# Sliding-window attention feeding a gated MLP: values cast by the loading DMA, attention outputs transposed by DMA

## The chip, the cores and the metric

The kernel runs on one core of a Trainium2 chip. The core has five engines with queues of their own: TensorE (PE, matrix products into PSUM), VectorE (DVE), ScalarE (ACT), GpSimd (POOL) and SyncE (SP, which here only issues DMAs). Sixteen DMA engines move data between HBM and SBUF; any of SyncE, ScalarE and GpSimd can issue to them. The metric is the device time of one execution in microseconds. The kernel before has a median of 345.35 us over three runs (345.25 to 346.49).

## The reference

There are 8 batches, 8 heads, 576 positions and a head size of 64. Attention is causal, sees the last 128 positions and carries a linear bias by distance with a slope for each head. Its output, one row of 512 numbers for each of the 4608 tokens, goes through two products with a gate between them.

```python
scores = scale * np.matmul(q, k.transpose(0, 1, 3, 2))
mask = (rel >= 0) & (rel < window)                     # window = 128
scores = np.where(mask, scores + bias[None], -1000000000.0)
attn = softmax(scores)                                 # written out in the reference
x = np.matmul(attn, v).transpose(0, 2, 1, 3).reshape(B * S, H * D)
# ---- then
h = x @ w_in                                           # 512 -> 2048
g = h * (1.0 / (1.0 + np.exp(-beta * h)))
out = g @ w_out                                        # 2048 -> 512
```

All inputs and the output are float32. The kernel computes its products in bfloat16 with float32 sums.

## The kernel before

The work is two streams that are woven together on TensorE. The attention stream goes batch by batch. A batch has five blocks of query positions (four of 128 and one of 64). The product stream goes in nine groups of 512 tokens: HS(g, j) makes one of 16 slices of the hidden layer, OS(g, i, n) a quarter of one of four output tiles. HS reads XT, a ring of three groups that holds the attention outputs with the features on the partitions.

Loads. Every block of q, k or v comes in as float32 by SyncE into a buffer of the pool `fst`, and GpSimd casts it to its place. Values land in VS, which is double-buffered by batch.

```python
fst_pool = ctx.enter_context(tc.tile_pool(name="fst", bufs=14))
bst_pool = ctx.enter_context(tc.tile_pool(name="bst", bufs=8))
xn_pool = ctx.enter_context(tc.tile_pool(name="xn", bufs=6))

def load_rows(src, b, sb):                  # 256 KB, rows of 256 bytes
    f = fst_pool.tile([P, H, D], F32, name="fst", tag="fst")
    nc.sync.dma_start(out=f[0:rows], in_=src[b, :, P*sb : P*sb+rows, :].rearrange("h p d -> p h d"))
    return f[0:rows]

def load_qk(b, sb):                         # batches 3 to 7
    t = bst_pool.tile([P, 2, H, D], BF16, name="bst", tag="bst")
    for i, src in enumerate((q, k)):
        c = nc.gpsimd.tensor_copy(out=t[0:ROWS[sb], i], in_=load_rows(src, b, sb))
    staged[b, sb] = t

def load_v(b, sb):
    return nc.gpsimd.tensor_copy(out=VS[b % 2][0:ROWS[sb], sb, :, 0:D], in_=load_rows(v, b, sb))
```

Transposes of q and k. In batches 0 to 2 TensorE does them. From batch 3 on TD does them by DMA, two for each block, issued by SyncE into QK, which is double-buffered by batch too.

```python
def TD(b, sb):
    src = staged.pop((b, sb))
    for i in range(2):
        nc.sync.dma_start_transpose(out=QK[b % 2][:, i, :, ...], in_=src[0:ROWS[sb], i]...)
```

Attention. SC(b, m, p) makes the scores of a pair of heads for one half of a batch and their exponentials. PV(b, qb, g) makes the weighted sum of values for four heads of block qb, and VectorE divides it. X(b, qb) turns the finished block onto XT: four transposes on TensorE, then a copy by VectorE (by ScalarE in batch 0), in two parts where the block crosses the end of the ring.

```python
def X(b, qb):
    xnv = xns.pop((b, qb))[:].rearrange("p h d -> p (h d)")
    tok0 = (b * S + P * qb) % XTR
    n1 = min(nq, XTR - tok0)
    parts = [(tok0, 0, n1)] + ([(0, n1, nq)] if n1 < nq else [])
    xt = psum_t.tile([P, NDM, P], BF16, name="xt", tag="t")
    for c in range(NDM):
        nc.tensor.transpose(out=xt[:, c, :], in_=xnv[:, c*P : (c+1)*P], identity=ident[:])
    copy = nc.vector.tensor_copy if b else nc.scalar.copy
    for at, r0, r1 in parts:
        copy(out=XT[:, :, at : at + r1 - r0], in_=xt[:, :, r0:r1])
```

The weave. TensorE's order is that of the program (a manual schedule). The order on the other engines, the DMA queue of SyncE among them, is made by a scheduler when the kernel is built; each queue is then served strictly in its order. `spread` puts the steps of a list `todo` between product steps, and leaves the last `tail` product steps without any. The `todo` of group g ends with the X that completes the tokens of group g+1. With tokens 0 to 2047 in groups 0 to 3, that is X(3, 2) for group 3.

```python
def spread(moe, todo, lead=0, tail=3): ...

def ahead(b, m):                # DMA issues, all at one place of the program
    def f():
        if m == 0:
            TD(b, 3), TD(b, 4); load_v(b, 2..4)
            if b + 1 < B: load_qk(b + 1, 0..2)
        elif b + 1 < B:
            TD(b + 1, 0..2); load_qk(b + 1, 3..4); load_v(b + 1, 0..1)
    return f

def by_block(b):                # batches 3 to 7; e is the batch before
    e = b - 1
    r = [pv(e, 2, 1), pv(e, 3, 1), x(e, 2), sc(b, 0, 0), x(e, 3), pv(e, 4, 1), sc(b, 0, 1),
         x(e, 4)] if e >= NTE else [sc(b, 0, 0), sc(b, 0, 1)]            # NTE = 3
    return [ahead(b, 0)] + r + [
        sc(b, 0, 2), pv(b, 0, 0), sc(b, 0, 3), pv(b, 1, 0), ahead(b, 1),
        pv(b, 0, 1), sc(b, 1, 0), x(b, 0), pv(b, 1, 1), sc(b, 1, 1), x(b, 1),
        sc(b, 1, 2), pv(b, 2, 0), sc(b, 1, 3), pv(b, 3, 0), pv(b, 4, 0)]

spread(hs(0), by_pair(1), 1, 0)             # batch 1 beside group 0
...                                         # hs(1) alone; batch 2 beside os(0) and half of os(1)
for g in range(2, NTG):                     # NTG = 9
    moe = ...                               # hs(g) with the rest of os(1), or with os(g - 1)
    if g + 1 < NTG:
        b, r = divmod(TOKG * (g + 2) - 1, S)
        end = todo.index(at[b, r // P]) + 1
    spread(moe, todo[done:end])
```

Output tiles are stored by GpSimd, those of the last group by SyncE.

Of the kernel before, what the change touches and what calls it, by code (L numbers as in the profile page):

```python
# [13 lines left out]
P = 128  # L14
# [3 lines left out]
def kernel(  # L18
# [10 lines left out]
    nc = tc.nc  # L29
    B, H, S, D = q.shape  # L30
# [8 lines left out]
    NTE = 3  # L39
# [36 lines left out]
    W2 = const.tile([P, NFF, DM], BF16, name="W2")  # L76
    const.seal()

    fst_pool = ctx.enter_context(tc.tile_pool(name="fst", bufs=14))
    bst_pool = ctx.enter_context(tc.tile_pool(name="bst", bufs=8))  # L80
    pt_pool = ctx.enter_context(tc.tile_pool(name="ptp", bufs=11))
    xn_pool = ctx.enter_context(tc.tile_pool(name="xn", bufs=6))
    gt_pool = ctx.enter_context(tc.tile_pool(name="gt", bufs=2))
    sig_pool = ctx.enter_context(tc.tile_pool(name="sig", bufs=3))
    osb_pool = ctx.enter_context(tc.tile_pool(name="osb", bufs=6))
# [37 lines left out]
    def load_qk(b, sb):  # L123
        t = bst_pool.tile([P, 2, H, D], BF16, name="bst", tag="bst")
        for i, src in enumerate((q, k)):
            c = nc.gpsimd.tensor_copy(out=t[0 : ROWS[sb], i], in_=load_rows(src, b, sb))  # L126
        staged[b, sb] = t
        return c

    def load_v(b, sb):  # L130
        return nc.gpsimd.tensor_copy(  # L131
            out=VS[b % 2][0 : ROWS[sb], sb, :, 0:D], in_=load_rows(v, b, sb)
        )
# [102 lines left out]
# [3 lines that stand above are left out]
            nc.sync.dma_start_transpose(  # L239
                out=QK[b % 2][:, i, :, P * sb : P * sb + ROWS[sb]],  # L240
                in_=src[0 : ROWS[sb], i].rearrange("r h d -> r (h d)"),
            )
# [80 lines left out]
    def X(b, qb):  # L323
        nq = ROWS[qb]
        xnv = xns.pop((b, qb))[:].rearrange("p h d -> p (h d)")
        tok0 = (b * S + P * qb) % XTR
        n1 = min(nq, XTR - tok0)
        parts = [(tok0, 0, n1)] + ([(0, n1, nq)] if n1 < nq else [])
        xt = psum_t.tile([P, NDM, P], BF16, name="xt", tag="t")
        for c in range(NDM):  # L330
            nc.tensor.transpose(  # L331
                out=xt[:, c, :], in_=xnv[:, c * P : (c + 1) * P], identity=ident[:]
# [4 lines that stand above are left out]
# [38 lines left out]
    def spread(moe, todo, lead=0, tail=3):  # L375
        done, n = 0, len(moe)
        for i, it in enumerate(moe):
            it()
            to = len(todo) * (i + 1 - lead) // (n - lead - tail)
            while done < min(len(todo), to):  # L380
                todo[done]()
                done += 1

    def sc(b, m, p):
        return lambda: SC(b, m, p)

    def pv(b, qb, g):
        return lambda: PV(b, qb, g)
# [6 lines left out]
    at = {}  # L395


    def ahead(b, m):
        def f():
            if m == 0:  # L400
                for sb in (3, 4):
                    TD(b, sb)
                for sb in (2, 3, 4):
                    load_v(b, sb)
                if b + 1 < B:
                    for sb in (0, 1, 2):
                        load_qk(b + 1, sb)
            elif b + 1 < B:
                for sb in (0, 1, 2):
                    TD(b + 1, sb)  # L410
                for sb in (3, 4):
                    load_qk(b + 1, sb)
                for sb in (0, 1):
                    load_v(b + 1, sb)
        return f

    def by_pair(b):
        return [
            lambda: TP(b, 0), lambda: TP(b, 1), sc(b, 0, 0), lambda: TT(b), sc(b, 0, 1),
            lambda: TP(b, 2), sc(b, 1, 0), lambda: TP(b, 3), sc(b, 1, 1), pv(b, 0, 0), sc(b, 0, 2),  # L420
            pv(b, 1, 0), sc(b, 1, 2), pv(b, 2, 0), sc(b, 0, 3), pv(b, 3, 0), sc(b, 1, 3),
            pv(b, 4, 0), pv(b, 0, 1), pv(b, 1, 1), x(b, 0), pv(b, 2, 1), x(b, 1), pv(b, 3, 1),
            x(b, 2), pv(b, 4, 1), x(b, 3), x(b, 4),
        ]

    def by_block(b):

        e = b - 1
        r = [pv(e, 2, 1), pv(e, 3, 1), x(e, 2), sc(b, 0, 0), x(e, 3), pv(e, 4, 1), sc(b, 0, 1),
             x(e, 4)] if e >= NTE else [sc(b, 0, 0), sc(b, 0, 1)]  # L430
        return [ahead(b, 0)] + r + [
            sc(b, 0, 2), pv(b, 0, 0), sc(b, 0, 3), pv(b, 1, 0), ahead(b, 1),
            pv(b, 0, 1), sc(b, 1, 0), x(b, 0), pv(b, 1, 1), sc(b, 1, 1), x(b, 1),
            sc(b, 1, 2), pv(b, 2, 0), sc(b, 1, 3), pv(b, 3, 0), pv(b, 4, 0),
        ]

    with tc.manual_schedule(engines={mybir.EngineType.PE}):

        for sb in range(NQB):
            c = load_v(0, sb)  # L440
            if sb == 3:
                with tc.issue_after(c.ins):
                    load_w1(0)
                    load_w1(1)
        for p in range(NP):
            c = load_pair(1, p, None if p else W1[0:1, 0, 0:1])
            if p % 2:
                with tc.issue_after(c.ins):
                    load_w1(2 + p // 2)
            if p == 1:  # L450
                load_tail(1)
        for sb in range(NQB):
            c = load_v(1, sb)
            if sb == 3:
                with tc.issue_after(c.ins):
                    for n in range(4):
                        load_w2(n)
        with tc.tile_pool(name="psum_x", bufs=2, space=bass.MemoryType.PSUM) as psum_x:
            pools = [psum_x, psum_x, psum_s]

            def sc0(m, p):
                SC(0, m, p, pools[0])
                pools.append(pools.pop(0))

            w = psum_t.tile([P, 512], F32, name="w", tag="t")
            idle(w[:], 9)
            TP(0, 0)
            TP(0, 1)
            sc0(0, 0)
            load_beta()  # L470
            TT(0)
            sc0(0, 1)
            TP(0, 2)
            sc0(1, 0)
            TP(0, 3)
            sc0(1, 1)
            for m in range(2):
                sc0(m, 2)
            for m in range(2):
                sc0(m, 3)  # L480
                PV(0, m, 0)
            for qb in (2, 3, 4):
                PV(0, qb, 0)
        psum_h = ctx.enter_context(
            tc.tile_pool(name="psum_h", bufs=2, space=bass.MemoryType.PSUM))
        psum_o = ctx.enter_context(
            tc.tile_pool(name="psum_o", bufs=2, space=bass.MemoryType.PSUM))
        w = psum_s.tile([P, 2, 512], F32, name="w", tag="sps")
        for qb in range(NQB):
            c = PV(0, qb, 1, (psum_o, "ops") if qb % 2 else (psum_h, "hps"))  # L490
            idle(w[:, 0, :], 1)
            if qb:
                X(0, qb - 1)
                idle(w[:, 1, :], 1)
        X(0, NQB - 1)
        with tc.issue_after(c.ins):
            late_consts()
        for p in range(NP):
            load_pair(2, p)
            if p == 1:  # L500
                load_tail(2)

        def hs(g):
            return [lambda j=j: HS(g, j) for j in range(NFF)]

        def os(g):
            return [lambda n=n: OS(g, n // 4, n % 4) for n in range(NFF)]


        spread(hs(0), by_pair(1), 1, 0)  # L510
        for sb in range(NQB):
            load_v(2, sb)
        for sb in (0, 1, 2):
            load_qk(3, sb)
        for it in hs(1):
            it()
        ahead(2, 1)()
        o1 = os(1)
        spread(os(0) + o1[0:8], by_pair(2))
        todo = sum((by_block(b) for b in range(NTE, B)), [])  # L520
        todo += [pv(B - 1, 2, 1), pv(B - 1, 3, 1), x(B - 1, 2), pv(B - 1, 4, 1), x(B - 1, 3),
                 x(B - 1, 4)]
        done = 0
        for g in range(2, NTG):
            moe = hs(g)
            if g == 2:
                moe = sum((moe[2 * n : 2 * n + 2] + [o1[8 + n]] for n in range(8)), [])
            else:
                moe = sum(([a, c] for a, c in zip(moe, os(g - 1))), [])
            end = len(todo)  # L530
            if g + 1 < NTG:
                b, r = divmod(TOKG * (g + 2) - 1, S)
                end = todo.index(at[b, r // P]) + 1
            spread(moe, todo[done:end])
            done = end
        for it in os(NTG - 1):
            it()
# [30 lines left out]
```

## Time and profile before

| | kernel before |
|---|---|
| time, median of 3 | 345.35 us |
| span of the profiled execution | 344.5 us |
| DMA queues of SyncE and ScalarE (hardware) | 119296 packets, 35.27 MB, 55.2% of 16 engines' span |
| DMA queue of GpSimd (software) | 6784 packets, 12.59 MB, 14.4% |
| transposes of attention outputs, TensorE (L331) | 160, 219 ns each |
| copies to XT, VectorE (L336) | 36, 13.8 us in all |
| casts of values, GpSimd (L131) | 40, 617 ns each |
| value loads, SyncE | 32 of 256 KB and 8 of 128 KB, 5.3 and 5.2 us to landing |
| transposes of q and k by DMA (L239) | 50, 3.2 us to landing |

A row of the page names a line of the kernel, an engine, an operation and its tiles as out<-in, then busy time, the mean of one, and the idle time of the engine before it with what ended it. "SPq" is the SyncE queue: the time there is that of issuing, not of the transfer. Matmuls overlap, so that the mean duration of one is longer than the distance between the starts of two.

### The profile page before, as it was taken

The numbers are of one execution on the slowest core, as the hardware profiler recorded it, in microseconds if no ns is written. First come the engines' busy times: TensorE is split into PE (matmuls) and PEld (weight loads), VectorE is DVE, ScalarE is ACT, GpSimd is POOL, SyncE is SP. The second block draws the span as 40 slices with busy tenths as digits, with TensorE's granted clock in tenths as the row PEclk, the third lists the DMA queues.
The fourth block names the chain that finished last, engine by engine and source line by source line (L and its number), as shares of the span: only waits on it lengthen the run. The fifth ranks groups of instructions, "written<-read, shape, count | busy, mean of one in ns | idle before, by whom it ended". The sixth has DMA issues, their size and how long they took to land.

```text
span 344.5 us, 6371 instructions
## 1 busy us (share of the span) xinstructions
PE 327.8 (95%) x2379; PEld 157.4 (46%) x2379; DVE 206.2 (60%) x447; ACT 211.5 (61%) x407; POOL 100.6 (29%) x173
## 2 busy tenths in 40 slices
PE   7988979999998999999999999999999999999995
PEld 2453434444453444444454444444544445444442
DVE  6476768776645785565677656676767456533300
ACT  4745754757618875667758774877587674444411
POOL 7635482250443434304804352200000000100000
PEclk9999999999999999999999999999999999999999
DMA  6999999999999999959999796100000000010021
GB/s 195 246 170 262 217 213 242 214 192 131 181 216 202 192 217 189 169 115 239 199 241 233 126 234 162 47 30 32 30 33 30 32 30 32 32 60 32 30 81 72
DMA packets 126143, 48.27 MB, mean 140 GB/s; under 512 B 113296, under 2 KB 123552, under 8 KB 126112
## 3 DMA queue, kind: packets, MB, share of 16 engines
q1 hardware_dynamic: 119296, 35.27, 55.2%
q0 software_dynamic: 6784, 12.59, 14.4%
q8 instruction: 18, 0.29, 0.4%
q14 instruction: 13, 0.11, 0.1%
q10 hardware_dynamic: 32, 0.01, 0.0%
HBM read 36.71 MB, written 9.44 MB: 134 GB/s over the span
## 4 chain that ended last, share of the span: by engine, by line
PE 71%; DMA 15%; SPq 5%; ACT 3%; DVE 3%; issue 1%; POOL 1%; POOLq 0%
PE ops L364 34%; PE hps L348 28%; DMA fst<-in_v_dram 7%; DMA fst<-in_k_dram 5%; PE sps L267 4%; SPq L95 3%; ACT pt L280 2%; SPq L109 2%; PE xt L331 2%; PE pv L311 2%; DMA W<-in_moe_w_in_dram 2%; DMA fst<-in_q_dram 2%; PE pv L307 1%; DVE pt L284 1%; DVE gT L354 1%
## 5 line engine op out<-in xcount | busy, mean ns | idle before, releaser
L348 PE MATMUL hps<-XT,W 128*128 128x512 bf16 x576 | 145.2, 379 | 0.6 <-DVE gT L354 0.4
L353 ACT ACTIVATE sig<-hps,beta_h 128x512 bf16<-128x512 f32 x144 | 99.6, 692 | 74.5 <-PE hps L348 67.1
L364 PE MATMUL ops<-W,gT 128*128 128x512 bf16 x576 | 145.0, 379 | 0.0
L354 DVE SCALAR_TENSOR_TENSOR gT<-sig,hps 128x512 bf16<-128x512 bf16 x144 | 98.4, 684 | 55.0 <-ACT sig L353 54.6
L280 ACT ACTIVATE pt<-sps,bias 128x256 bf16<-128x256 f32 (+1 forms) x192 | 75.2, 477 | 14.3 <-PE sps L267 13.9
L348 PEld LDWEIGHTS <-W 128*128 128x128 bf16 x576 | 51.3, 97 | 57.1 <-issue 4.8
L364 PEld LDWEIGHTS <-gT 128*128 128x128 bf16 x576 | 51.3, 98 | 52.5 <-issue 1.5
L126 POOL CAST bst<-fst 128x512 bf16<-128x512 f32 (+1 forms) x50 | 32.2, 646 | 57.3 <-DMA fst<-in_q_dram 38.9
L372 POOL DMA_DIRECT2D out_dram<-osb x32 | 17.4, 543 | 107.4 <-ACT osb L370 107.4
L284 DVE TENSOR_TENSOR pt<-pt,mask 128x1024 bf16<-128x1024 bf16 x48 | 35.2, 733 | 17.5 <-ACT pt L280 17.0
L370 ACT ACTIVATE osb<-ops 128x512 f32<-128x512 f32 x36 | 21.7, 602 | 25.8 <-PE ops L364 25.8
L131 POOL CAST vs<-fst 128x512 bf16<-128x512 f32 (+1 forms) x40 | 24.5, 617 | 43.2 <-DMA fst<-in_v_dram 32.2
L317 DVE TENSOR_TENSOR xn<-pv,zs 128x256 bf16<-128x256 f32 (+1 forms) x80 | 33.6, 422 | 2.4
L311 PE MATMUL pv<-vs,pt 128*128 128x65 bf16 x320 | 28.2, 193 | 2.3 <-POOL vs L131 2.3
L267 PE MATMUL sps<-qkT 64*128 64x256 bf16 (+2 forms) x320 | 25.2, 252 | 2.9 <-ACT pt L280 2.9
L316 DVE RECIPROCAL zs<-pv 128x4 f32<-128x4 f32 (+1 forms) x80 | 14.1, 178 | 22.6 <-PE pv L311 21.9
L311 PEld LDWEIGHTS <-pt 128*128 128x128 bf16 x320 | 21.8, 97 | 9.9 <-issue 0.8
L307 PE MATMUL pv<-vs,pt 128*128 128x65 bf16 x256 | 24.4, 193 | 1.5 <-DVE xn L317 0.8
L267 PEld LDWEIGHTS <-qkT 64*128 64x128 bf16 x320 | 10.9, 94 | 30.3 <-issue 29.5
L307 PEld LDWEIGHTS <-pt 128*128 128x128 bf16 x256 | 19.9, 98 | 10.2 <-issue 3.2
L336 DVE COPY XT<-xt 128x512 bf16<-128x512 bf16 (+1 forms) x36 | 13.8, 389 | 14.4 <-PE xt L331 13.7
L275 ACT ACTIVATE pt<-sps 128x1024 bf16<-128x1024 f32 x16 | 16.0, 1027 | 10.1 <-PE sps L267 10.0
(44 smaller groups left out, 125.3 us busy)
## 6 DMA issues: line engine op xcount, KB each, us to landing
fst<-in_q_dram SPq DMA_DIRECT2D x32, 256.0 KB, 5.2
fst<-in_k_dram SPq DMA_DIRECT2D x32, 256.0 KB, 5.2
fst<-in_v_dram SPq DMA_DIRECT2D x32, 256.0 KB, 5.3
out_dram<-osb POOLq DMA_DIRECT2D x32, 256.0 KB, 3.0
W<-in_moe_w_in_dram POOLq DMA_DIRECT2D x4, 512.0 KB, 7.4
W<-in_moe_w_out_dram POOLq DMA_DIRECT2D x4, 512.0 KB, 12.6
fst<-in_q_dram SPq DMA_DIRECT2D x8, 128.0 KB, 5.1
fst<-in_k_dram SPq DMA_DIRECT2D x8, 128.0 KB, 4.8
```

The lines of the kernel that those rows point to most:

```text
L126: c = nc.gpsimd.tensor_copy(out=t[0 : ROWS[sb], i], in_=load_rows(src, b, sb))
L131: return nc.gpsimd.tensor_copy(out=VS[b % 2][0 : ROWS[sb], sb, :, 0:D], in_=load_rows(v, b, sb))
L267: nc.tensor.matmul(o, lhsT=qk[64 * e : 64 * e + 64, 1, p, P * kb : P * kb + P], rhs=qk[64 * e : 64 * e + 64, 0, p, P * kb : P * kb + nq], ...
L280: nc.scalar.activation(out=pt[:, e, cols], in_=sps[:, e, cols], func=ACTF.Exp, scale=qscale, bias=bias[:, half, h : h + 1],)
L284: nc.vector.tensor_tensor(out=pt[:], in0=pt[:], in1=masks[m][:].rearrange("p (o c) -> p o c", o=1).broadcast_to([P, 2, 512]), op=ALU.mult,)
L307: nc.tensor.matmul(pv[:, hl, 0 : D + 1], lhsT=weights(b, qb - 1, h, 1), rhs=vs[:, qb - 1, h, 0 : D + 1], start=True, stop=False,)
L311: nc.tensor.matmul(pv[:, hl, 0 : D + 1], lhsT=weights(b, qb, h, 0), rhs=vs[:, qb, h, 0 : D + 1], start=qb == 0, stop=True,)
L317: nc.vector.tensor_tensor(out=xn[0:nq, 4 * g : 4 * g + 4, :], in0=pv[0:nq, :, 0:D], in1=zs[0:nq].broadcast_to([nq, 4, D]), op=ALU.mult,)
L348: nc.tensor.matmul(hps[:], lhsT=W1[:, c, bass.ts(j, P)], rhs=XT[:, c, c0 : c0 + TOKG], start=(c == 0), stop=(c == NDM - 1),)
L353: nc.scalar.activation(out=sig[:], in_=hps[:], func=ACTF.Tanh, scale=beta_h[:, j : j + 1])
L354: nc.vector.scalar_tensor_tensor(out=gts[g][:, j, :], in0=sig[:], scalar=1.0, in1=hps[:], op0=ALU.add, op1=ALU.mult)
L364: nc.tensor.matmul(ops_[:], lhsT=gT[:, j, i * P : i * P + P], rhs=W2[:, j, :], start=(j == 0), stop=(j == NFF - 1),)
```

## The change

For batches 3 to 7, values are loaded by a GpSimd DMA that casts on the way and writes straight into VS, so that there is no buffer in `fst`, no SyncE issue and no cast on GpSimd. X for these batches is one DMA transpose from the normalised block to XT (two where the block crosses the end of the ring), issued by SyncE; TensorE, PSUM and VectorE are not used for it. The DMA issues that `ahead` made at one place are placed one at a time between the attention steps. `fst` has one buffer less, `xn` two more; the batch-1 steps start two product steps later; from group 3 on the last six product steps of a group have no attention steps between them. It is meant to take work off TensorE, VectorE and GpSimd and to smooth the DMA issues.

```diff
-    fst_pool = ctx.enter_context(tc.tile_pool(name="fst", bufs=14))
+    fst_pool = ctx.enter_context(tc.tile_pool(name="fst", bufs=13))
-    xn_pool = ctx.enter_context(tc.tile_pool(name="xn", bufs=6))
+    xn_pool = ctx.enter_context(tc.tile_pool(name="xn", bufs=8))
...
     def load_v(b, sb):
+        if b >= NTE:
+            nc.gpsimd.dma_start(
+                out=VS[b % 2][0 : ROWS[sb], sb, :, 0:D],
+                in_=v[b, :, P * sb : P * sb + ROWS[sb], :].rearrange("h p d -> p h d"),
+            )
+            return
...
     def X(b, qb):
+        if b >= NTE:
+            for at, r0, r1 in parts:
+                nc.sync.dma_start_transpose(out=XT[:, :, at : at + r1 - r0], in_=xnv[r0:r1, :])
+            return
...
-    def ahead(b, m):
-        def f(): ...
+    def ahead(b, m, r):
+        td = [lambda c=c, sb=sb: TD(c, sb) for c, sb in (
+            ((b, 3), (b, 4)) if m == 0 else ((b + 1, 0), (b + 1, 1), (b + 1, 2)))]
+        qk = [lambda sb=sb: load_qk(b + 1, sb) for sb in ((0, 1, 2), (3, 4))[m]]
+        vs = [lambda sb=sb: load_v(b + m, sb) for sb in ((2, 3, 4), (0, 1))[m]]
+        ...                                  # td, then vs and qk (m = 0) or qk and vs (m = 1)
+        n, k, out = len(r), 0, []
+        for i, f in enumerate(r):
+            out.append(f)
+            while k < len(ops) and k * n <= i * len(ops):
+                out.append(ops[k])
+                k += 1
+        return out + ops[k:]
...
-        return [ahead(b, 0)] + r + [
-            sc(b, 0, 2), pv(b, 0, 0), sc(b, 0, 3), pv(b, 1, 0), ahead(b, 1),
+        r += [sc(b, 0, 2), pv(b, 0, 0), sc(b, 0, 3), pv(b, 1, 0)]
+        t = [
             pv(b, 0, 1), sc(b, 1, 0), x(b, 0), pv(b, 1, 1), sc(b, 1, 1), x(b, 1),
             sc(b, 1, 2), pv(b, 2, 0), sc(b, 1, 3), pv(b, 3, 0), pv(b, 4, 0),
         ]
+        return ahead(b, 0, r) + ahead(b, 1, t)
...
-        spread(hs(0), by_pair(1), 1, 0)
+        spread(hs(0), by_pair(1), 3, 0)
...
-            spread(moe, todo[done:end])
+            spread(moe, todo[done:end], 0, 3 if g == 2 else 6)
```

More of the change, by code (lines that the diff above doesn't have):

```diff
@@ L395 @@
     at = {}
-    def ahead(b, m):
[L399 to L415, printed above, removed]
+    def ahead(b, m, r):
[3 more added lines that the diff above has]
+        vs = [lambda sb=sb: load_v(b + m, sb) for sb in ((2, 3, 4), (0, 1))[m]]
+        ops = vs if m == 0 else []
+        if b + 1 < B:
+            ops = td + (vs + qk if m == 0 else qk + vs)
+        elif m == 0:
+            ops = td + vs
+        n, k, out = len(r), 0, []
[5 more added lines that the diff above has]
+        return out + ops[k:]
     def by_pair(b):
@@ L516 @@
             it()
-        ahead(2, 1)()
+        for f in ahead(2, 1, [lambda: None]):
+            f()
         o1 = os(1)
```

## The prediction, made before the changed kernel ran

> **What bounds the kernel now.** I read the page first, then the windows by stage, then the timelines of TensorE and of the SyncE queue, to see which engine is ahead of which.
>
> ```profile
> PE 327.8 (95%) x2379; PEld 157.4 (46%) x2379; DVE 206.2 (60%) x447; ACT 211.5 (61%) x407; POOL 100.6 (29%) x173
> ...
> DMA  6999999999999999959999796100000000010021
> ```
>
> TensorE is busy 95% of the span, and the DMA engines are full from about 8 to 200 us (slices of 8.6 us), then nearly empty. The windows cut at the first matmul of the fourth token group (133.3 us) show where TensorE still waits:
>
> ```profile
> 66.00:133.30 67.30, 62.89 (x504) 31.09 (x503) 45.32 (x94) 43.25 (x94) 26.30 (x44) 1.00 1.07 192
> 133.30:215.00 81.70, 81.70 (x583) 38.65 (x582) 51.61 (x107) 55.95 (x115) 30.61 (x51) 1.00 1.04 190
> 215.00:344.50 129.50, 125.81 (x795) 59.14 (x793) 64.63 (x127) 72.87 (x140) 9.36 (x17) 0.99 0.11 40
> ```
>
> The columns are window, length, busy time of PE, PEld, DVE, ACT and POOL, clock, DMA share, GB/s. From 133.3 us on TensorE has no idle time before its tail, so work taken off it there is time saved. The DMA share is above 1 until 215 us and 0.11 after that. In the second window the full DMAs cost nothing, because what they bring is wanted much later: the queue runs ahead with batches 5 to 7. TensorE at this point:
>
> ```profile
> 130.48 0.40 PE L331 MATMUL xt<-ident,xn 128*128 128x128 bf16 x4 [0.49 <-DVE xn L317]
> 130.72 1.89 PE L348 MATMUL hps<-XT,W 128*128 128x512 bf16 x8
> 132.44 1.03 PE L364 MATMUL ops<-W,gT 128*128 128x512 bf16 x4
> 133.31 1.03 PE L348 MATMUL hps<-XT,W 128*128 128x512 bf16 x4
> ```
>
> The four transposes of an attention output start at 130.48 us and the next matmul at 130.72: they cost 0.24 us of issue, not 0.40. This is block 2 of batch 3, and 133.31 us is HS(3,0), which needs its columns of XT. Now the SyncE queue:
>
> ```profile
> 131.71 5.91 SPq L239 DMA_TRANSPOSE qkT<-bst  x4
> ...
> 181.03 1.25 SPq L95 DMA_DIRECT2D fst<-in_q_dram  x1
> 182.38 1.42 SPq L95 DMA_DIRECT2D fst<-in_k_dram  x1
> ...
> 187.52 8.72 SPq L239 DMA_TRANSPOSE qkT<-bst  x6
> ```
>
> The first line is TD(5,0) and TD(5,1). They needed only the score matmuls of batch 3, half 0, which TensorE issued by 111.5 us, yet the queue came to them at 131.71: it is already 20 us behind TensorE. Today that harms nothing.
>
> **What the Trainium skill says.** "DMA: Bandwidth & Descriptors", section "Issuing engines are not separate DMA queues": DMAs issued from SyncE, ScalarE or GpSimd share the same 16 engines. The DMA row agrees in that it is full; so I take moving values to GpSimd to free SyncE issue time, not DMA time. "Advanced Engine Details and Errata", section "X-Bar Transpose (TRN2)": transposing DMAs are as fast as regular ones. Here that isn't so as issued: four 128 KB transposes take 5.91 us of the queue, against about 1.2 us for each 256 KB load, so the measurement decides. "TensorE: Matmul & The Clock Gate", section "Part 4: PE-mode transpose", has about 275 ns for one transpose in a kernel; the trace has 219 ns duration and 56 to 60 ns of spacing, and only spacing counts here. The same page, section "Part 1: The HAM clock gate", has the array at half clock after an idle window and for about 3.4 us of new work. The first matmuls of this trace agree (9 warm-up matmuls in 4.02 us, 0.43 us each, where 0.22 is the later spacing).
>
> **The change, part by part.**
>
> 1. TensorE: 25 blocks (five in each of batches 3 to 7) lose 4 transposes: 100 spacings that sum to 5.87 us in the trace (0.235 a block). Three of these blocks lie before 133.3 us (0.7 us), 22 after it (5.2 us). All on the path.
> 2. VectorE: 26 copies of XT leave (one block is split at the ring's end), 26 x 0.4 = 10 us. VectorE is at 60%: nothing.
> 3. GpSimd: 25 value casts of 0.617 us leave (15 us); 25 DMA issues come, which I estimate at 1 us from the 0.54 us of an output store and 0.77 us of a weight load. At 29% busy: nothing.
> 4. SyncE: 25 value loads leave, 26 transposes of 1.2 to 1.3 us come. What counts is where they stand. TensorE's order is written by hand, the queue's is made by the scheduler, and the built order of the changed kernel has, around the first of them (batch numbers are mine):
>
> ```
> 6 loads batch 6, 4 TD(5,0..1), 2 loads batch 6,
> XT(3,0), 2 loads batch 6, XT(3,1), 3 loads batch 7,
> 6 TD(5,2..4), 2 loads batch 7,
> XT(3,2), XT(3,3), 5 loads batch 7, XT(3,4), 4 TD(6,0..1) ...
> ```
>
> HS(3,0) now waits for XT(3,2), which stands in a queue served in order behind q and k of batches 3 to 6 and half of batch 7, and behind 30 TD. In the kernel before, the queue is past the same loads at 182.38 us (the k load there comes just after them). The scheduler evidently supposes a faster DMA than the chip has.
>
> 5. When does the queue reach XT(3,2)? Both kernels are alike until the q load of batch 3 at 66.03 us. From there the kernel before takes 182.4 - 66.0 = 116.4 us for 45 q/k loads, 20 value loads (18 full ones' worth) and 34 TD. The changed queue has no value loads, and 30 TD plus 2 XT, two fewer. Taking 18 x 1.13 = 20 us and 2 x 1.3 = 2.6 us away gives 94 us, or 160 us on the clock, if values cost nothing. But those of batches 3, 4 and part of 5 (some 12 full loads, 13.6 us) still pass the same DMA engines. Part of that fits in the holes that bursts of transposes leave: while the queue issues them at 1.3 us apiece, each lands within 0.5 us of the last if the engines are backed up, so the engines run dry. Between 157 and 172; I choose an issue at 162 us and a landing at 166, with 3.2 us the median and 6.0 the longest landing of a TD.
> 6. HS(3,0) then starts at 166 instead of 132.6 us (133.3 less the 0.7 of point 1): a wait of 33 us.
> 7. From HS(3,0) to the end the kernel before takes 344.5 - 133.3 = 211.2 us. Minus 5.2 (point 1), plus 2.2 for matmuls at half clock after the wait (about ten of them at 0.43 instead of 0.22), is 208.2. The later groups should not wait: by then all loads are issued, and the spread now ends 6 steps (6 x 0.87 = 5.2 us) before each next group, against about 1 us on VectorE, one or two issues of 1.3 us and a landing of 2.4 us. End: 166 + 208.2 = 374.2 us of span. The times lie 0.9 us above the profiled span (345.35 and 344.5): 375 us.
>
> The fst pool of 13 instead of 14 and the later start of the second batch's attention I take as zero: four to five loads are in flight in this stage (landing 5.2 us, one each 1.2 us), and the shift changes order, not work.
>
> **Rivals.**
>
> A. The transfer is hidden: XT arrives in time, and the 5.9 us of point 1 come out, with perhaps 1 us of waits on pooled PSUM that vanish. That makes 338.5 to 340 us. For it: TensorE is without a gap in the second half, and SyncE loses 25 issues. Against it: XT(3,2) would have to be issued by about 129 us. Pure issue cost from 66 us (45 x 0.6 for a load that is not pushed back, 32 x 1.3) is 69 us, that is 135 us, and it is reached only if the DMA engines never push back, which they do throughout this stage.
>
> B. A small wait: GpSimd's queue fills the holes so well that DMA work alone bounds. That work, from 66 us: 41 full q/k loads x 1.13, 12 values x 1.13, 32 transposes x 0.5 and 8 output stores x 0.7 (64 packets of some 190 ns over 16 engines) = 82 us, so an issue at 148, landing at 152, a wait of 19 us, and 361 us in all.
>
> C. A larger one: casting packets write 128 bytes each and may be slower than the 256-byte ones; the queue also waits for GpSimd's casts, which now stand behind value DMAs that wait for TensorE to be done with batches 1 to 3. Ten more microseconds make 385 to 388 us.
>
> D. Each later group waits too, 1 to 3 us, because XT passes a queue that TD(6) or TD(7) holds for 5 to 8 us. With the DMAs idle and 5.2 us of room I expect under 2 us in all.
>
> **Range and chances.** 375 us lies between B (361) and C (388). I stretch the low end to 354, as the queue's lag may shrink further without value loads. A has about one chance in eight, and it ends at the edge of 2% (338.4 us), so a gain of over 2% gets 0.05 and within 2% 0.10. Slower has 0.85.
>
> **What would show it.** TensorE should have one idle stretch of 15 to 45 us just before HS(3,0), ended by the landing of XT<-xn, with the granted clock at half afterwards. The chain of waits should pass there from TensorE to DMA XT<-xn, and to SyncE loads before it. XT(3,0), ready at about 118 us, should be issued near 145. Past it TensorE should be dense, with HS(3,0) to the end at about 208 us. L331 should fall from 160 to 60 matmuls. The prediction is wrong if XT(3,2) is issued before 135 us (rival A), or if waits are spread over all groups (rival D), or if the loss lies ahead of 130 us.

## The result

| | kernel before | changed kernel |
|---|---|---|
| time, median of four runs on one chip | 345.7 us | 382.59 us (380.56 to 383.06) |
| ratio, 95% interval | | 1.1053, 1.1005 to 1.1101 |
| span of the profiled execution | 344.5 us | 380.3 us |
| HS(3,0) starts | 133.3 us | 169.84 us |
| from HS(3,0) to the end | 211.2 us | 210.4 us |

The change costs 36.9 us, and nearly all of it is one wait of TensorE. In the page of the changed kernel (busy time first, then slices of 9.5 us, then the chain of waits by engine, then a group of matmuls with its idle time):

```profile
PE 322.1 (85%) x2236; PEld 153.4 (40%) x2279; DVE 195.0 (51%) x421; ACT 211.1 (56%) x407; POOL 105.2 (28%) x173
...
PE   6988988998989900019999999999998999999996
...
PEclk9899999999999955559999999999999999999999
...
DMA  8899999998999998999371985492111111201012
...
PE 56%; DMA 22%; SPq 10%; ACT 4%; POOL 3%; issue 3%; DVE 2%; POOLq 0%
...
L358 PE MATMUL hps<-XT,W 128*128 128x512 bf16 x556 | 143.6, 381 | 38.4 <-DMA XT<-xn 37.2
```

VectorE has 26 instructions less and TensorE is idle for three slices in a row and most of a fourth. The idle time stands at the HS matmuls and was ended by the landing of XT<-xn. The granted clock falls to half in that gap. The trace lacks about forty matmul records (556 of 576 in this group), so I time stages by their first matmul and not by counts. The windows, with the columns of the prediction's:

```profile
66.00:132.00 66.00, 61.89 (x487) 30.80 (x494) 44.07 (x92) 43.40 (x96) 29.36 (x46) 1.00 1.19 181
132.00:170.00 38.00, 0.81 (x5) 0.23 (x3) 1.06 (x2) 1.11 (x2) 15.38 (x25) 0.54 1.18 180
170.00:218.00 48.00, 47.58 (x308) 21.54 (x313) 26.83 (x54) 31.78 (x65) 11.44 (x18) 0.97 0.65 102
218.00:380.30 162.30, 155.18 (x956) 71.79 (x973) 79.57 (x157) 95.99 (x188) 15.01 (x25) 1.00 0.30 62
```

In the second window no compute engine but GpSimd has anything to do, and the DMA share is 1.18: the DMA engines are full, mostly with what belongs to later batches. The timeline of TensorE shows the gap itself:

```profile
131.63 1.03 PE L374 MATMUL ops<-W,gT 128*128 128x512 bf16 x4
169.84 1.89 PE L358 MATMUL hps<-XT,W 128*128 128x512 bf16 x4 [37.19 <-DMA XT<-xn]
```

The timeline of the SyncE queue shows what it was doing meanwhile:

```profile
146.84 1.52 SPq L337 DMA_TRANSPOSE XT<-xn  x1
...
149.87 1.26 SPq L337 DMA_TRANSPOSE XT<-xn  x1
151.23 0.53 SPq L95 DMA_DIRECT2D fst<-in_q_dram  x1
151.86 0.96 SPq L95 DMA_DIRECT2D fst<-in_k_dram  x1
152.91 2.16 SPq L95 DMA_DIRECT2D fst<-in_q_dram  x1
155.17 8.97 SPq L245 DMA_TRANSPOSE qkT<-bst  x6
164.24 0.53 SPq L95 DMA_DIRECT2D fst<-in_k_dram  x1
164.86 0.53 SPq L95 DMA_DIRECT2D fst<-in_q_dram  x1
165.49 3.53 SPq L337 DMA_TRANSPOSE XT<-xn  x2
```

The first line is XT(3,0). VectorE had its block ready at 117.30 us, so it stood in the queue for 29.5 us. XT(3,2) is the first of the two in the last line. It was issued at 165.49 and landed at 169.80, and HS(3,0) began 0.04 us later. Between the two stand XT(3,1), loads of batch 7 and TD(5,2) to TD(5,4); TensorE needed none of these loads and TD yet. The block of XT(3,2) was finished by this instruction of VectorE, at 130.49 us:

```profile
130.07 0.42 DVE L323 TENSOR_TENSOR xn<-pv,zs 128x256 bf16<-128x256 f32 x1
```

So the wait of 37.2 us is 35.0 us in the queue and 4.3 us of landing, less the 2.2 us from there to the end of TensorE's other work (132.65 us). Only the 35.0 us belong to the place in the queue.

### The profile page after: what moved, and what is told of

Same layout as the page of the kernel before. It is cut to its first block, busy times and chain, and to the rows that moved or that the text cites. A ratio compares the mean times of both kernels' runs of the same rounds, so it can differ in the third digit from the quotient of the medians.

```text
span 380.3 us, 6165 instructions
## 1 busy us (share of the span) xinstructions
PE 322.1 (85%) x2236; PEld 153.4 (40%) x2279; DVE 195.0 (51%) x421; ACT 211.1 (56%) x407; POOL 105.2 (28%) x173
## 4 chain that ended last, share of the span: by engine, by line
PE 56%; DMA 22%; SPq 10%; ACT 4%; POOL 3%; issue 3%; DVE 2%; POOLq 0%
PE ops L374 28%; PE hps L358 22%; DMA fst<-in_k_dram 10%; DMA fst<-in_v_dram 7%; SPq L245 4%; SPq L95 3%; PE sps L273 3%; ACT pt L286 3%; SPq L109 2%; PE pv L317 2%; DMA W<-in_moe_w_in_dram 1%; POOL bst L126 1%; DMA qkT<-bst 1%; PE pv L313 1%; DMA XT<-xn 1%
## 5 line engine op out<-in xcount | busy, mean ns | idle before, releaser
L358 PE MATMUL hps<-XT,W 128*128 128x512 bf16 x556 | 143.6, 381 | 38.4 <-DMA XT<-xn 37.2
L374 PE MATMUL ops<-W,gT 128*128 128x512 bf16 x557 | 142.8, 380 | 1.0 <-issue 0.2
L374 PEld LDWEIGHTS <-gT 128*128 128x128 bf16 x576 | 52.6, 98 | 58.1 <-issue 3.4
L290 DVE TENSOR_TENSOR pt<-pt,mask 128x1024 bf16<-128x1024 bf16 x48 | 33.9, 707 | 33.2 <-ACT pt L286 33.1
L126 POOL CAST bst<-fst 128x512 bf16<-128x512 f32 (+1 forms) x50 | 30.7, 624 | 64.4 <-DMA fst<-in_k_dram 31.1
L132 POOL DMA_DIRECT2D vs<-in_v_dram x25 | 21.3, 853 | 33.7 <-PE pv L317 32.1
L113 POOL CAST bst<-fst 128x512 bf16<-128x512 f32 x24 | 14.7, 622 | 11.6 <-DMA fst<-in_q_dram 6.1
```

The lines of the kernel that those rows point to most:

```text
L290: nc.vector.tensor_tensor(out=pt[:], in0=pt[:], in1=masks[m][:].rearrange("p (o c) -> p o c", o=1).broadcast_to([P, 2, 512]), op=ALU.mult,)
L358: nc.tensor.matmul(hps[:], lhsT=W1[:, c, bass.ts(j, P)], rhs=XT[:, c, c0 : c0 + TOKG], start=(c == 0), stop=(c == NDM - 1),)
L374: nc.tensor.matmul(ops_[:], lhsT=gT[:, j, i * P : i * P + P], rhs=W2[:, j, :], start=(j == 0), stop=(j == NFF - 1),)
```

## The experiments

My theory is that the whole loss is the place of XT(3,2) in a queue that is served in order, behind loads that run ahead. The rivals are that the DMA engines have too much to move whatever the order, that casting value packets are slow (rival C of the prediction), and that every group waits a little (rival D). In the diffs `VDMA` and `XDMA` are the first batch whose values, or attention outputs, go by the new DMA; in the changed kernel both conditions read `NTE`, which is 3. The kernel before ran again beside each group of experiments (medians of 345.38 to 345.78 us), and each ratio is to those runs. Runs over 1.5% above the fastest of the same kernel, one in experiment 6 and four in experiment 8, are left out of the ratios.

**1. The transposes back on TensorE.** The other parts of the change stay.

```diff
-VDMA, XDMA = 3, 3
+VDMA, XDMA = 3, 8
```

> The changed kernel with X on TensorE again for all batches; values still loaded by the casting GpSimd DMA, issues still spread. Theory (HS(3,0) waits because XT(3,2) stands behind loads in SyncE's queue): the wait of 37 us is gone and so is the saving of 5.9 us; 345 us, 342 to 349. Rival (casting value DMAs slow the DMA engines so that TensorE waits for q, k or values): still over 355 us.

Measured: 349.74 us (348.35 to 350.37), ratio 1.0121 (1.0091 to 1.0150). No wait for XT is left, and 32.9 us of the 36.9 are gone. This part of the loss comes with the DMA transposes. The time is 0.7 us above the expected range: about 4 us that I had not expected stay, so something else in the change costs too (experiments 4 to 6).

**2. SyncE in program order.** The queue is no longer ordered by the scheduler, so XT(3,2) stands behind 50 q and k loads and 18 TD, instead of 75 and 30.

```diff
-    with tc.manual_schedule(engines={mybir.EngineType.PE}):
+    with tc.manual_schedule(engines={mybir.EngineType.PE, mybir.EngineType.SP}):
```

> The changed kernel with SyncE's queue too held to the order of the program, nothing else changed: XT(3,2) now stands behind 50 q/k loads and 18 TD instead of 75 and 30. Theory (order of the queue): HS(3,0) waits under 3 us and the saving on TensorE shows; 341 us, 337 to 347. Rival (the 16 DMA engines are too full whatever the order): a wait of 15 us or more before HS(3,0), over 355 us.

Measured: 355.43 us (354.0 to 356.54), ratio 1.0288 (1.0255 to 1.0322). The edit names nothing but the order of SyncE, and 27 us come back; the wait before HS(3) falls from 37.2 to 4.7 us. The built order of GpSimd's casts and DMA issues moves with it, so the two are not varied apart here. The DMA engines have as much to move in all as before, so what counts is the order. The size is a miss: 341 was expected. The timeline of the SyncE queue of this kernel shows why:

```profile
100.81 3.05 SPq L245 DMA_TRANSPOSE qkT<-bst  x2
117.82 1.68 SPq L337 DMA_TRANSPOSE XT<-xn  x1
119.60 5.31 SPq L245 DMA_TRANSPOSE qkT<-bst  x4
125.01 1.21 SPq L337 DMA_TRANSPOSE XT<-xn  x1
...
133.13 1.21 SPq L337 DMA_TRANSPOSE XT<-xn  x1
```

The queue stood still from 103.9 to 117.82 us, with XT(3,0) at its head waiting for its block. Then four TD, four loads and two more TD had to go out before XT(3,2) at 133.13, which landed at 137.68. The block of XT(3,2) was ready at 130.95 us, so 2.2 us of the 4.7 lie in the queue; the rest is a landing of 4.6 us against the room of 2.2 us before HS(3). What else makes 355 out of 341 I can place only in part: the 4 us of experiments 4 to 6, a second wait for XT of 2.0 us before HS(5), some half clock after the first wait, and transposes that are worth less than expected (point 1 below). An order with XT too far ahead stops the queue as one with XT too far behind stops TensorE.

**3. Values back on SyncE, outputs by DMA.**

```diff
-VDMA, XDMA = 3, 3
+VDMA, XDMA = 8, 3
```

> The changed kernel with values loaded by SyncE and cast by GpSimd as before; attention outputs still transposed by DMA. In the built order XT(3,2) stands behind 60 q/k loads, 30 value loads and 30 TD, which the kernel before has behind it at 154.5 us. Theory (order of the queue): issue near 157 us, landing 161, a wait of 28 us, 373 us in all, 365 to 380, so less than the changed kernel. Rival (the casting DMAs relieve SyncE, without them the queue is later still): 395 us or more.

Measured: 374.78 us (372.11 to 375.95), ratio 1.0825 (1.0776 to 1.0874); as expected, and the rival is out. The wait before HS(3), in the waits of this kernel (total, times, longest):

```profile
PE hps L359 <- DMA XT<-xn: 26.8, 2, 26.4
```

By count, XT(3,2) has as long a queue ahead of it as in the changed kernel: 60 q and k loads, 30 value loads and 30 TD here, 75, 15 and 30 there. Yet it lands at 161.45 instead of 169.80 us, 8.4 us earlier. From 66 us to the issue of XT(3,2), SyncE's queue moved 56719 packets of 256 bytes here and 56527 there; in the changed kernel GpSimd's queue moved 11903 packets of its casting DMAs besides, whose time is 24.3 us of all 16 engines together. SyncE's waits for GpSimd's casts do not differ: 16.8 us here and 16.2 us there, from 66 to 166 us. So I put the 8.4 us down to those packets: the two parts make each other worse. It is argued from the traces; no run varies these packets alone.

**4. Neither DMA part.** What is left is the spread of the issues, the pools, the lead of three and the tail of six.

```diff
-VDMA, XDMA = 3, 3
+VDMA, XDMA = 8, 8
```

> The changed kernel with both kinds of DMA undone: values loaded by SyncE and cast by GpSimd, X on TensorE for all batches; what stays is the spread of issues, the pool sizes and the places of the attention steps (batch 1 two steps later, six product steps without attention from group 3 on). Theory (the 4 us by which the kernel with X on TensorE is slower than the kernel before come from the places of the steps, the casting value DMAs are hidden): 348.5 us, 347 to 351. Rival (they come from the casting value DMAs): 344.5 to 346.

Measured: 350.07 us (349.48 to 350.44), ratio 1.0127 (1.0104 to 1.0149). With the values by casting DMA (experiment 1) it was 1.0121, within the intervals; the time lies in the expected range. So where nothing waits for the SyncE queue, the casting DMAs cost nothing and gain nothing, and the 4 us are in the weave.

**5. The lead back to one.** Experiment 4 with one number changed:

```diff
-        spread(hs(0), by_pair(1), 3, 0)
+        spread(hs(0), by_pair(1), 1, 0)
```

> The changed kernel without its two DMA parts, and with the batch-1 steps starting one product step in, as before, instead of three; fst, xn, the spread issues and the tail of six stay. Theory (the lead costs): the stretch from HS(0) to HS(1) falls from 32.3 to about 30.5 us, and the time from 350.1 to 348.3 us, range 347.5 to 349. Rival (the later start costs nothing, the 32.3 us has another cause): the time stays within 0.5 us of 350.1.

Measured: 348.11 us (347.81 to 349.27), ratio 1.0069 (1.0052 to 1.0086). So the lead costs 2.0 us, as expected. The traces show where: HS(1) starts at 58.97 us in experiment 4 (first line, timeline from 57 to 61 us) and at 56.96 here (second line, from 55 to 59 us).

```profile
58.97 2.32 PE L359 MATMUL hps<-XT,W 128*128 128x512 bf16 x10
56.96 2.32 PE L359 MATMUL hps<-XT,W 128*128 128x512 bf16 x10
```

It starts at 56.5 to 57.1 us in the seven kernels with a lead of one and at 57.8 to 60.3 in the seven with three. The stretch from HS(0) to HS(1), which the expectation named, falls from 32.28 to 30.57 us, but is a poor measure: it is 32.34 in the kernel before, with a lead of one and an earlier HS(0). The rest lies after HS(3): 213.9 us from there to the end, against 211.2 in the kernel before. The waits of TensorE in that stretch (from 133 us) show what it is; the kernel before has none there:

```profile
PE pv L318 <- DVE pt L291: 1.5, 3, 0.6
PE sps L274 <- ACT pt L287: 0.7, 1, 0.7
```

With six product steps kept free at the end of each group, the attention steps are packed closer and wait for ScalarE and VectorE: 2.2 us. Experiment 6 varies the tail alone.

**6. DMA transposes from batch 5 on, with a tail of six and of three.** XT(5,0) stands behind all 80 q and k loads, which are out by then.

```diff
-VDMA, XDMA = 3, 3
+VDMA, XDMA = 3, 5
```

> The changed kernel with DMA transposes to XT only from batch 5 on (15 blocks); batches 3 and 4 on TensorE. In the built order the first of them, XT(5,0), stands behind all loads, which end near 175 us, and it is wanted near 190 us. Theory: no wait over 2 us at any group and 15 x 0.235 = 3.5 us saved; 342 us, 339 to 346. Rival (each group waits for its last DMA transpose): 1 to 3 us at four groups, 346 us or more.

Measured: 347.12 us (344.49 to 348.4), ratio 1.0041 (1.0019 to 1.0063). No group waits for XT. The time is a miss, 1.1 us above the range, for the lead and the tail were not in it; the rival's waits did not come. Then the tail alone:

```diff
-            spread(moe, todo[done:end], 0, 3 if g == 2 else 6)
+            spread(moe, todo[done:end], 0, 3)
```

> As the kernel with DMA transposes from batch 5 on, but the attention steps of every group spread until three product steps before its end, as in the kernel before, instead of six. Theory (the six cost some 3 us by packing the steps, and buy off 1 to 2 us of waits for late DMA transposes): 346 us, 344 to 347.5. Rival (the six are needed): 349 us or more.

Measured: 344.64 us (343.54 to 350.2), ratio 0.9970 (0.9952 to 0.9987). Three steps are room enough for these late groups, for there is still no wait for XT, and 2.5 us come back, as in experiment 5. This version is faster than both kernels, by 0.3% than the kernel before.

**7. The kernel before with outputs by DMA for batches 6 and 7 alone**, and nothing else of the change.

```diff
+        if b >= 6:
+            for at, r0, r1 in parts:
+                nc.sync.dma_start_transpose(out=XT[:, :, at : at + r1 - r0], in_=xnv[r0:r1, :])
+            return
```

> The kernel before with one thing changed: attention outputs of batches 6 and 7 (10 blocks) transposed by DMA. The queue is free of loads from about 203 us and these are wanted from 230 us on. Theory: 10 x 0.235 = 2.35 us saved, about 1 us given back before the last group; 344 us, 342.5 to 345.5.

Measured: 344.19 us (343.32 to 345.01), ratio 0.9956 (0.9940 to 0.9972): the lowest median of all versions, 1.5 us below the kernel before, though its interval overlaps that of the second kernel of experiment 6. Ten blocks at 0.235 us would be 2.35. No group waits for XT, so the 1 us that was to be given back is not there.

**8. The kernel before with both DMA parts from batch 5 on** (lead one, tail three, issues at one place).

```diff
+        if b >= 5:              # in load_v: the casting DMA of the change
...
+        if b >= 5:              # in X: the transposing DMA of the change
```

> The kernel before with attention outputs of batches 5 to 7 (15 blocks) transposed by DMA, and the values of the same batches loaded by the casting GpSimd DMA, so that 15 loads leave the queue ahead of them. Theory: 3.5 us saved, 1.4 us given back before group 5 (two half transposes) and 1 us before the last group; 344.2 us, 342.5 to 346. Rival (XT(5,1) still comes too late): a wait of over 5 us before group 5, 348 us or more.

Measured: 345.5 us in the 18 runs that count (346.1 in all 22, from 343.82 to 352.38), ratio 0.9997 (0.9978 to 1.0015). The wait of 1.2 us before group 5 is there as expected. It takes a third of what 15 blocks could give (15 x 0.235 = 3.5 us), and no gain can be measured. The time is above what was expected, 344.2 us.

**9. Issues at one place, with 13 and with 14 buffers in `fst`.** Both DMA parts from batch 3 on, but no spread, lead one, tail three.

```diff
+    fst_pool = ctx.enter_context(tc.tile_pool(name="fst", bufs=13))     # 14 in the second kernel
+    xn_pool = ctx.enter_context(tc.tile_pool(name="xn", bufs=7))
+        if b >= NTE:            # both DMA parts, as in the change
```

> The kernel before with both DMA parts (values cast by the GpSimd DMA, attention outputs transposed by DMA, batches 3 to 7), 13 buffers in fst and 7 in xn; the DMA issues stand at one place again, the lead is one step and the tail three. In the built order XT(3,2) stands behind 73 q and k loads and 30 TD (75 and 30 in the changed kernel). Theory (the place in the queue sets the wait, and the spreading of the issues has no part in it): HS(3) waits 33 to 37 us, and without the lead and the tail the time is 377 us, range 372 to 381. Rival (spreading one issue per step is what pushed the loads in front): a wait under 20 us and a time under 365 us.

> The same as one_place_f13 with one buffer more in fst (14, as in the kernel before) and no other edit. The built order differs: XT(3,2) stands behind 56 q and k loads and 26 TD instead of 73 and 30, since the q and k of batch 6 and half of 7 now come after it. Theory (the place in the queue sets the wait): at about 0.66 us for a load and 1.3 us for a TD, 17 loads and 4 TD less are 16 us, so HS(3) waits about 19 us (10 to 23) and the time is 361 us, range 351 to 366. Rival (the wait is set by what the DMA engines have to move or by the transposes themselves): the wait stays above 28 us and the time within 5 us of one_place_f13.

Measured: 376.3 us (376.25 to 379.46), ratio 1.0900 (1.0866 to 1.0934), with 13 buffers; 376.95 us (374.28 to 378.38), ratio 1.0910 (1.0877 to 1.0944), with 14. The waits of the first kernel, with 13 buffers:

```profile
PE hps L360 <- DMA XT<-xn: 33.3, 1, 33.3
```

And those of the second, with 14:

```profile
PE hps L360 <- DMA XT<-xn: 32.7, 1, 32.7
```

The first expectation holds, and spreading the issues had no part in the loss. The second one does not: it rests on another place of XT(3,2), and the traces show that place to be wrong. In both kernels the queue issues the same things in the same order, 73 q and k loads, 15 value loads and 30 TD ahead of XT(3,2). So this pair does not vary the place in the queue. It shows only that one buffer more or less in `fst` does nothing.

**10. Loads and TD held behind XT.** Both DMA parts from batch 3 on; the q and k loads and the TD of batches 5 to 7 may enter the queue only after XT(b-2, 2), where that one already stands ahead of them in the program. The tail is six ahead of group 3 and three elsewhere.

```diff
     def load_qk(b, sb):          # and TD in the same way
+        after = xdma.get((b - 2, 2))       # the DMA that X(b - 2, 2) issued, if it did
+        if after is None:
+            return load_qk_now(b, sb)
+        with tc.issue_after(after.ins):
+            return load_qk_now(b, sb)
```

> The kernel before with both DMA parts for batches 3 to 7, 7 buffers in xn, lead one, the issues at one place, a tail of six ahead of group 3 alone, and one edit more: the q and k loads and the TD of batches 5 to 7 are put in the queue only after XT(b-2, 2). In the built order XT(3,0), XT(3,1) and XT(3,2) stand behind 56 q and k loads and 20 TD (73 to 75 and 30 without the hold), and XT(4,1) behind 66 and 30. Theory (the place of XT in a queue served in order is the whole loss): TD(4) ends at about 121 us, so XT(3,2) is issued as soon as its block is ready, about 129 us, lands by 134, HS(3) waits 0 to 3 us, and most of the 5.9 us of the transposes remains: 343 us, range 340.5 to 346. Rival (the DMA engines are full and the held loads come too late for batches 5 to 7, so that the wait is only moved to a later group): 350 us or more, with waits on qkT or XT after group 4.

Measured: 361.51 us (359.18 to 364.32), ratio 1.0447 (1.0410 to 1.0484). Both sides are half right. The wait before HS(3) falls to 4.0 us: XT(3,2) was issued at 130.54 us and landed at 136.41, 5.9 us later (the DMA share from 130.5 to 136.5 us is 1.39). But the wait came back behind it, 9.8 us before HS(5) and 3.7 before HS(6). In the waits of this kernel (total, times, longest):

```profile
PE hps L376 <- DMA XT<-xn: 17.5, 3, 9.8
```

In the timeline of its SyncE queue:

```profile
163.39 18.58 SPq L353 DMA_TRANSPOSE XT<-xn  x3
182.07 2.54 SPq L261 DMA_TRANSPOSE qkT<-bst  x2
...
207.88 3.18 SPq L353 DMA_TRANSPOSE XT<-xn  x2
```

The first line holds XT(4,0), XT(4,1) and XT(4,2). The last of them went out at 180.76 us, when its block was ready (180.70); the queue had stood at it from 166.9 us on. From 182 us on ten TD and ten loads had to pass before XT(5,1) in the last line. Its first part landed at 213.39 and let HS(5) begin at 213.53. Holding the loads moves the same conflict two groups on.

## Why the prediction was right, point by point

The time (382.59 against 375) lies inside the range, and its central step, one wait of TensorE before HS(3,0) for a transpose stuck in the SyncE queue, is what the trace shows.

- *Point 1, TensorE.* Right in kind, too large. A block was to be worth 0.235 us; from experiment 4 to 6, 15 blocks are worth 350.07 - 347.12 = 2.95 us (0.20 each), and in experiment 7 ten are worth 1.5 us (0.15 each; 0.19 by the traces, where HS(3) to HS(8) takes 165.9 us before and 164.0 there). Before HS(3,0) the work ended at 132.65 us (169.84 - 37.19), against the 132.6 chosen, and that is luck: HS(2,0) starts 1.2 us later than before (104.21 and 103.04 us), and the stretch from there is 1.8 us shorter, not 0.7.
- *Points 2 and 3, VectorE and GpSimd: nothing.* Right. The value DMAs took 0.853 us of GpSimd each, against the estimate of 1, and GpSimd is at 28%. In the groups and the DMA issues of the page:

```profile
L132 POOL DMA_DIRECT2D vs<-in_v_dram x25 | 21.3, 853 | 33.7 <-PE pv L317 32.1
...
vs<-in_v_dram POOLq DMA_DIRECT2D x20, 128.0 KB, 4.8
```

- *Point 4, the queue.* Right. Experiment 2 changes that order and takes 32.5 of the 37.2 us of wait away.
- *Point 5, when the queue reaches XT(3,2).* Chosen 162 out of 157 to 172, measured 165.49; the landing took 4.3 us where 4 were taken. This mis-sized term, 3.8 us with the landing, is half of the error of 7.6. I gave the value DMAs an effect of 2 us, on top of the 160 us at which the queue would be there without them; experiment 3, with an equally long queue and no such DMAs, is there at 158.16 us, 7.3 us before the changed kernel. So the queue alone was taken too slow and the value DMAs too cheap, and the two errors partly cancel. The 1.13 us for a load that the sum rests on is not derived there; in the kernel before the queue took 1.23 us for each of the eight loads from 155.21 to 165.06 us.
- *Point 6, the wait.* 37.2 us instead of 33, from point 5.
- *Point 7, the rest.* 210.4 us instead of 208.2. The half clock lasted for six matmul spacings of 0.43 us, 6 x 0.21 = 1.3 us instead of 2.2. "The Trainium skill", page "TensorE: Matmul & The Clock Gate", section "Part 1: The HAM clock gate", puts the slow start at about 3.4 us; here it was some 2.6. What the sum had left out is the cost of the tail of six, 2.2 us of waits and 2.5 us of time (experiments 5 and 6): I had counted it as room for the transfer and not as attention steps that are packed closer. The distance between time and span was 2.3 us instead of 0.9, the last part of the error: each sets a median of runs beside the span of one execution, and within the execution that was profiled it is 1.8 us in both kernels.
- *`fst` and the lead, taken as zero.* Right for `fst` (experiment 9). Wrong for the lead: 2.0 us by itself (experiment 5). In the changed kernel it lies ahead of the wait, which swallows it.
- *Rival A* is out: the wait that it took as none is 37.2 us. It had no room either: the block was ready at 130.49 us, so that even an empty queue would, with the landing of 4.3 us, have left a wait of 2.2. *Rival B* had the right direction, but its issue at 148 us and its wait of 19 us are both about 18 us short. *Rival C:* its ingredient is there. The packets of the casting DMAs took 33.0 ns on average for 128 bytes each, those of 256 bytes 23.2 ns, so that the values of five batches cost 23040 x 9.8 ns / 16 = 14 us more of all DMA engines together. But experiments 1 and 4 show that they cost no time of their own; they count only where something waits for the queue. Its other half, a queue held up by GpSimd's casts, is not what happened (16.2 us of such waits, 16.8 in experiment 3). *Rival D* is out: no later group of the changed kernel waits for XT.

The span adds up as follows. HS(3,0) starts 36.5 us later, and what comes after it is 0.8 us shorter. That is 35.7 of the 35.8 us by which the spans differ. In experiment 4, which has the tail of six and no DMA part, that last stretch is 214.0 us, 2.8 us longer than before; the changed kernel's is 3.5 us shorter than that. With 1.3 us for the clock, the transposes of 22 blocks saved 4.8 us (0.22 each) instead of 5.2.

What stays open: why a block's transposes are worth 0.15 to 0.22 us and not the 0.235 of their spacing, and whether an order exists that gets all five batches' outputs through one queue without a stop at either end. Moving the loads to another queue, so that SyncE has the transposes alone, was not tried.

## What to carry to other kernels

Before work on the critical path moves to a DMA, look at the queue that will issue it: how far is it ahead of or behind the engine that waits, and what stands in front of the new entry in the order that was built? Here a queue that ran ahead was harmless as long as nothing in it was wanted soon; one entry that TensorE waited for at once turned the entries before it into latency (35.0 us), and one put too early stopped those behind it (14 us in experiment 2). In this kernel such a transfer paid only where the prefetches were over, for the last two or three batches, and there it gave 0.3 to 0.4% (experiments 6 and 7) or nothing that can be measured (experiment 8).

## What the runs showed that I had not expected

- A reserve is not free. Six product steps instead of three at the end of each group cost 2.5 us in experiment 6 and took no wait for XT away: the kernel with three had none either.
- A GpSimd DMA of 128 KB with a cast took 0.853 us of the engine, and the cast that it replaces 0.617 us (15.4 us for 25): it took more of GpSimd, not less.
- With an equally long SyncE queue, an entry of it landed 8.4 us later where GpSimd's queue moved values besides (experiment 3).
- Naming the order of one queue by hand moved the built order of another: GpSimd's is not the same in experiment 2 as in the changed kernel.
